# Another order of the same steps in a landmark-attention and two-MLP kernel on one core

## The chip, the core and the metric

The kernel runs on one core of one Trainium2 chip. The metric is the device time of one execution in microseconds (us). The engines are TensorE (PE; its weight loads are shown as PEld), VectorE (DVE), ScalarE (ACT), GpSimd (POOL) and SyncE (SP, which issues the loads). Each engine works off its own queue of instructions in the order in which they were issued, and waits on semaphores for the others.

## What is computed

Landmark attention over 4 batches of 8 heads (576 positions, width 64), then a gated MLP, then an MLP with Mish:

```python
q_lm, k_lm = mean over 18 positions each of q, k          # 32 landmarks
A, Bm, C = sm(q, k_lm), sm(q_lm, k_lm), sm(q_lm, k)        # sm: softmax of scaled scores
Z = Bm.T / (norm1(Bm) * norminf(Bm) + 1e-6)
for _ in range(6):
    Z = 2 * Z - Z @ Bm @ Z
x = (A @ Z @ C @ v)                                        # 2304 tokens x 512
h = ((x @ w1) * (x @ w2)) @ w3 @ w_out                     # 1024 wide
g = mish(h @ w_in)                                         # 2048 wide
out = g @ w_out2
```

## The kernel before

Weights come from memory as 64-bit floats and are decoded on the chip to 32 bits. Everything ahead of the Mish part is cut into 1614 named steps. Each step is declared once with its engine, the steps that it must follow, the buffers that it takes and frees, and a function that emits its instructions. The string `ORDER` (lines 24 to 148) lists the names in one sequence; `issue()` walks it, gives each step the buffer that was freed first, and emits it. So `ORDER` sets the order of each engine's queue, which step gets which buffer, and, where a step has a choice (`@ACT`, `@DVE`, `@POOL`), on which engine it runs. A step whose buffer was used before waits for the last step that used it. The Mish part (`p2`, `z_mm`, `o_mm`, `tick`) comes after the string and is not in it.

The names, with the lines that carry them:

- `ld u` loads a weight tile (512 KB of 64-bit words) into one of seven raw buffers, on SP. It is decoded by `da` (top bits, ACT line 201 or DVE line 203), `dm` (sign, DVE line 207), `ds` (rescale, ACT line 210) and `db` (join, DVE line 214). `wo0` to `wo7` and `w30` to `w315` are the output and the third weight of the gated MLP, `w000` to `w171` its first and second, `x0` to `x25` those of the Mish part. `hi` and `lo` split a tile into a rounded part and a rest.
- `mm n x` multiplies a tile of w3 with one of wo (line 356, two matmuls); sixteen n of four x make the product w3 @ w_out in eight accumulators. Only two banks serve these until the last `mm`, so `mm 4 0` takes the bank of the first accumulator, which `ehi 0` (ACT) and `elo 0` (DVE, line 223) empty, and so on for `mm 8` and `mm 12`.
- `lk`, `lq`, `lv` load K, Q and V of a batch. `ks`, `qs` sum over 18 positions: for batch 0 on DVE (`ks3`, `qs3`, `ks4`, `qs4`, line 409), for the others on POOL as a tree of adds (lines 417, 420, 423). `bdk0` to `bdq3` (lines 432, 434) lay the sums out for the scores.
- A: `as` scores (line 450), `amx`, `asb`, `aex`, `asm`, `aad`, `arc`, `amul` the softmax, `atr` transposes (line 506), `ahi`, `alo` the split (line 223). C: `cs` scores (line 528), `cm`, `cex`, `cad`, `crc`, `ctr`, `cev`, `cv` (line 587), `cve`. Bm and its inverse: `bs` (line 611) to `btr`, `ns0` to `npy1`, then `bp` and `nm`, `nu` in turn (line 646 on TensorE, line 703 on DVE). `lt` and `lte` make Z @ C @ v. The number after the space is the batch. Five banks are shared by `as`, `cs`, `atr`, `ctr`, `cv` and `lt`; one serves `bs`, `bp` and `nm`.
- `m b s` folds that into w1 and w2 for 128 columns (line 850), with `mh`, `ml` splitting it; `xa`, `xb` multiply with A (lines 189 to 191, three matmuls for each product of split parts), `xc` and `xm` (line 886) multiply the two. `sh`, `sl` split the result, `y u m` multiplies with w3 @ w_out (24 matmuls, half a batch u), `ye` copies it out. `yh`, `yl` split it for the Mish part. `swap` ends the attention's buffers.

## Time and profile before

| | us |
|---|---|
| median of 3 runs | 779.53 (776.64 to 779.83) |
| the profiled execution | 776.88 |
| its span in the trace | 775.1 |
| TensorE busy | 750.3 (97%) |
| DVE busy | 350.4 (45%) |
| ACT busy | 337.6 (44%) |
| POOL busy | 120.1 (15%) |

The views used are the page (busy time, the chain that ended last, the groups), the busy time and granted TensorE clock of single stretches, and the instructions of one engine in order of time. A clock of 1.00 is the upper of its two levels (2.4 GHz), 0.50 the lower (1.2 GHz); a value between is a stretch with both. In a line of the order of time, the bracket says how long the engine stood idle ahead of it and what ended that. Ends of matmuls are modelled, so neighbours overlap a little in the list. Times are from the span's start.

### The profile page before, as it was taken

What the parts mean: (1) busy time and instruction counts of PE and PEld (TensorE: products, weight loads), DVE (VectorE), ACT (ScalarE), POOL (GpSimd) and SP (SyncE); (2) the same over time, 40 slices, a digit from 0 to 9 for tenths busy, and PEclk for the clock granted to TensorE, in tenths of its full rate; (3) what the DMA queues carried; (4) which work ended last, traced back from release to release, by engine and by line L of the source; (5) the groups of instructions that cost most, each with busy time, mean ns of one, the idle gap of its engine ahead of it and who ended that gap; (6) DMA issues with size and microseconds to landing.
All of it is one profiled execution on the core that took longest, in us unless ns stands there. A gap on an engine that the chain in (4) does not pass through costs nothing.

```text
span 775.1 us, 13036 instructions
## 1 busy us (share of the span) xinstructions
PE 750.3 (97%) x5188; PEld 616.3 (80%) x5188; DVE 350.4 (45%) x706; ACT 337.6 (44%) x737; POOL 120.1 (15%) x120
## 2 busy tenths in 40 slices
...
GB/s 312 369 329 106 80 192 167 256 127 83 117 114 72 110 55 98 140 117 137 30 107 28 1 0 55 1 0 1 55 0 1 1 0 55 1 0 1 55 1 27
DMA packets 38381, 65.92 MB, mean 85 GB/s; under 512 B 3888, under 2 KB 20400, under 8 KB 38320
## 3 DMA queue, kind: packets, MB, share of 16 engines
...
## 4 chain that ended last, share of the span: by engine, by line
PE 91%; DVE 5%; DMA 2%; issue 1%; ACT 1%; POOL 0%; SPq 0%; DVEq 0%; POOLq 0%
PE ps L189 26%; PE ps L191 26%; PE ps L190 26%; PE ps L356 6%; PE ps L850 2%; PE ps L450 1%; DVE raw L207 1%; DMA raw<-in_wo_dram 1%; PE ps L646 1%; DVE raw L214 1%; PE ps L528 1%; PE ps L587 1%; DMA k<-in_kT_dram 1%; PE ps L566 1%; PE ps L506 0%
## 5 line engine op out<-in xcount | busy, mean ns | idle before, releaser
L1101 ACT ACTIVATE emx<-ps 128x512 f32<-128x512 f32 (+1 forms) x80 | 44.3, 554 | 131.6 <-PE ps L191 131.6
L1103 DVE TENSOR_TENSOR gx<-emx,gx 128x512 fp32r<-128x512 f32 (+1 forms) x40 | 25.6, 639 | 158.6 <-ACT gx L1102 158.6
L189 PE MATMUL ps<-hs,W 128*128 128x288 f32 (+2 forms) x304 | 92.7, 305 | 0.0
L190 PE MATMUL ps<-hs,W 128*128 128x288 f32 (+2 forms) x304 | 92.4, 304 | 0.0
L191 PE MATMUL ps<-hs,W 128*128 128x288 f32 (+2 forms) x304 | 92.2, 303 | 0.0
L207 DVE TENSOR_SCALAR raw<-raw 128x512 uint16<-128x512 uint16 x84 | 74.4, 917 | 37.6 <-ACT raw L201 37.2
L1103 DVE TENSOR_TENSOR hs<-emx,hs 128x512 fp32r<-128x512 f32 (+1 forms) x40 | 25.6, 639 | 136.6 <-ACT hs L1102 136.6
L189 PE MATMUL ps<-AT,M 128*128 128x288 f32 x256 | 78.3, 306 | 1.0 <-DVE M L223 0.9
L190 PE MATMUL ps<-AT,M 128*128 128x288 f32 x256 | 75.6, 295 | 0.0
L191 PE MATMUL ps<-AT,M 128*128 128x288 f32 x256 | 75.5, 295 | 0.0
L210 ACT ACTIVATE raw<-raw 128x512 f32<-128x512 f32 x84 | 55.8, 678 | 29.8 <-DVE raw L207 25.6
L356 PE MATMUL ps<-wo,raw 128*128 128x512 f32 x128 | 61.9, 643 | 5.7 <-DVE raw L214 5.7
L201 ACT ACTIVATE raw<-raw 128x512 int32<-128x512 uint16 x79 | 52.7, 673 | 24.2 <-DMA raw<-in_w_dram 10.5
L190 PEld LDWEIGHTS ps<-hs,W 128*128 128x128 f32 x304 | 57.5, 189 | 1.4
L189 PEld LDWEIGHTS ps<-hs,W 128*128 128x128 f32 x304 | 57.1, 188 | 1.8 <-ACT y L218 0.4
L191 PEld LDWEIGHTS ps<-hs,W 128*128 128x128 f32 x304 | 57.5, 189 | 1.2
L356 PEld LDWEIGHTS ps<-wo,raw 128*128 128x128 f32 x128 | 26.6, 212 | 38.2 <-issue 28.6
L189 PEld LDWEIGHTS ps<-AT,M 128*128 128x128 f32 x256 | 48.1, 188 | 8.2 <-issue 2.1
L1102 ACT ACTIVATE gx<-ps 128x512 fp32r<-128x512 f32 (+1 forms) x40 | 22.2, 556 | 61.2 <-PE ps L190 61.2
L190 PEld LDWEIGHTS ps<-AT,M 128*128 128x128 f32 x256 | 48.1, 188 | 0.0
L191 PEld LDWEIGHTS ps<-AT,M 128*128 128x128 f32 x256 | 48.1, 188 | 0.0
L1102 ACT ACTIVATE hs<-ps 128x512 fp32r<-128x512 f32 (+1 forms) x40 | 22.3, 557 | 54.7 <-PE ps L190 54.7
...
## 6 DMA issues: line engine op xcount, KB each, us to landing
raw<-in_w_dram SPq DMA_DIRECT2D x128, 128.0 KB, 2.6
raw<-in_wo_dram SPq DMA_DIRECT2D x22, 512.0 KB, 4.4
...
raw<-in_wi_dram SPq DMA_DIRECT2D x14, 512.0 KB, 3.9
...
```

The costliest lines, as they stand in the source:

```text
L189: T.matmul(out=o, lhsT=lh, rhs=rh, start=first, stop=False)
L190: T.matmul(out=o, lhsT=lh, rhs=rl, start=False, stop=False)
L191: T.matmul(out=o, lhsT=ll, rhs=rh, start=False, stop=last)
L201: S.activation(w[..., 0], q[..., 1], ACTF.Copy, scale=2.0 ** -13, bias=2.0 ** -14 - 0.5)
L207: V.tensor_scalar(q[..., 1], q[..., 3], 0x8000, None, op0=ALU.bitwise_and)
L210: S.activation(f32(w[..., 1]), f32(w[..., 1]), ACTF.Copy, scale=2.0 ** -112)
L214: V.scalar_tensor_tensor(to, w[..., 1], 3, w[..., 0], op0=ALU.logical_shift_left, op1=ALU.bitwise_or)
L356: T.matmul(out=got(f"acc{i}"), lhsT=f32(got(f"w3{n}")[:, o:o + 128, 0]), rhs=WO0[j // 4][:, j % 4], start=j == 0, stop=j == 7)
L850: T.matmul(out=got(f"p{c}{key}")[32 * i:32 * i + 32, 0:256], lhsT=LT[r, b, 2 * c + par, :], rhs=w12(f"w{bp}{s}{c}")[r, par * 256:par * 256 ...
L1101: S.activation(x, zt[n], ACTF.Mish)
L1102: S.activation(gb(n, 0), zt.pop(n), ACTF.Mish)
L1103: V.tensor_tensor(gb(n, 1), x, f32(gb(n, 0)), op=ALU.subtract)
```

## The change

The string `ORDER` is replaced. The 1614 steps are the same, with the same work in each and the same rules of what must follow what; their sequence is another from the 21st on, and 35 of them run on another engine: 20 `lo` and 7 `sl` go from POOL to DVE, 2 `sl` from DVE to POOL, 2 `sh` from ACT to POOL, `da wo6` from DVE to ACT, `da x6` from ACT to DVE, and `bdq1 3` and `bdq2 3` change places on ACT and POOL. As buffers are given out in the order of the string, many steps also get another bank or buffer. SP's loads are the same; of the first 36, `lk0 2` and `lk1 2` come ahead of `ld w34`, and `lv 1` ahead of `ld w36`. The `y` of the first two batches (u = 0 to 3, but for the last of them, `y 3 3`) now come ahead of `m 2 2`, where before `y 2` and `y 3` stood behind all `xa`; `y 3 3` and `y 4` to `y 7` come behind them.

The sequence at the start, at the first `y`, where `m 2 2` stands, and at the end:

```diff
-    "da wo0@ACT,dm wo0,da wo1@ACT,ds wo0,dm wo1,db wo0,ds wo1,da w30@ACT,ld wo5,db wo1,dm w30,da wo2@ACT,ld w32,"
-    "ds w30,dm wo2,db w30,ds wo2,da wo3@ACT,mm 0 0,db wo2,dm wo3,da w31@ACT,mm 0 1,ds wo3,dm w31,mm 0 2,db wo3,"
-    "ds w31,da wo4@ACT,mm 0 3,ld wo6,ld wo7,db w31,dm wo4,mm 1 0,ld w33,ks3 0,ds wo4,mm 1 1,db wo4,mm 1 2,qs3 0,"
-    "mm 1 3,ks4 0,ld w34,ld w35,bdk0 0@ACT,bdk1 0@ACT,qs4 0,bdk2 0@ACT,bdk3 0@ACT,as0 0,bdq0 0@ACT,bdq1 0@ACT,"
-    "bdq2 0@ACT,bdq3 0@ACT,bs 0,amx0 0,cs0 0,bmx 0,bsb 0,asb0 0,by 0,cs1 0,bsm 0,aex0 0,bad 0,brc 0,bml 0,btr 0,"
-    "ns0 0,bp 0,ns1 0,lk0 2,lk1 2,nc 0,as1 0,ntr 0,nx 0,nml 0,nad 0,nrc 0,npy0 0,npy1 0,cm00 0,nm0 0,cm10 0,nu0 0,"
-    "cm20 0,nm1 0,cm01 0,ks0 1,cex00 0,nu1 0,cm11 0,cex10 0,nm2 0,cm21 0,as2 0,nu2 0,cex01 0,amx1 0,cex11 0,nm3 0,"
-    "asb1 0,lq0 2,lq1 2,ctr0 0,ks1 1,nu3 0,aex1 0,asm0 0,ctr1 0,da wo5@ACT,amx2 0,nm4 0,ks2 1,asm1 0,cev00 0,"
-    "nu4 0,ks3 1,cev10 0,asb2 0,nm5 0,da w32@ACT,ks4 1,cv0 0,nu5 0,dm wo5,aex2 0,cev01 0,dm w32,ds wo5,da wo6@DVE,"
-    "ds w32,db wo5,cev11 0,da wo7@ACT,cv1 0,db w32,ld w36,bdk0 1@ACT,lv 1,bdk1 1@ACT,dm wo6,mm 2 0,bdk2 1@ACT,"
-    "da w33@ACT,dm wo7,mm 2 1,ds wo6,dm w33,ds wo7,db wo6,mm 2 2,ds w33,db wo7,da w34@ACT,mm 2 3,db w33,ld w37,"
-    "ld w38,da w35@ACT,dm w34,mm 3 0,ld w39,bdk3 1@ACT,dm w35,ds w34,mm 3 1,cad0 0,ds w35,db w34,mm 3 2,crc0 0,"
-    "qs0 1,asm2 0,cve0 0,mm 3 3,ehi 0,elo 0,lt0 0,ehi 1,ld w310,as0 1,qs1 1,lte0 0,elo 1,db w35,mm 4 0,cad1 0,"
-    "crc1 0,qs2 1,amx0 1,cve1 0,mm 4 1,aad0 0,arc0 0,qs3 1,aad1 0,da w36@ACT,arc1 0,mm 4 2,amul0 0,mm 4 3,dm w36,"
...
-    "bsm 1,cm00 1,bdk2 2@ACT,bdk3 2@ACT,cm10 1,cm20 1,mm 8 1,qs1 2,asb0 1,cex00 1,amx1 1,mm 8 2,cex10 1,asb1 1,"
-    "qs2 2,aex0 1,mm 8 3,amx2 1,aex1 1,qs3 2,asm0 1,mm 9 0,ld w315,qs4 2,asm1 1,bdq0 2@ACT,mm 9 1,db w312,"
...
-    "ml1 2 2,xa 3 1 0,sl 0 7@DVE,sh 1 2@POOL,xm 2 1 0,xb 3 1 0,dm w150,sh 1 3@POOL,xc 2 1 1,y 0 0,ds w150,dm w151,"
...
-    "ld x24,ld x25,da x22@ACT,dm x22,y 7 0,yh 0,yh 1,yl 0,yh 2,yl 1,yh 3,yl 2,da x23@ACT,yl 3,da x24@ACT,dm x23,"
-    "y 7 1,ds x22,dm x24,da x25@ACT,db x22,ds x23,dm x25,ds x24,db x23,y 7 2,ds x25,db x24,ye 6 3,ye 7 0,db x25,"
-    "ye 7 1,y 7 3,ye 7 2,ye 7 3"
...
+    "da wo0@ACT,dm wo0,da wo1@ACT,ds wo0,dm wo1,da w30@ACT,db wo0,ds wo1,dm w30,ld wo5,da wo2@ACT,db wo1,ds w30,"
+    "dm wo2,ld w32,da wo3@ACT,db w30,ds wo2,dm wo3,mm 0 0,da w31@ACT,db wo2,ds wo3,mm 0 1,dm w31,da wo4@ACT,"
+    "mm 0 2,db wo3,ds w31,dm wo4,mm 0 3,ld wo6,ld wo7,ks3 0,ds wo4,ld w33,qs3 0,ks4 0,db w31,bdk0 0@ACT,"
+    "bdk1 0@ACT,qs4 0,bdk2 0@ACT,mm 1 0,bdk3 0@ACT,mm 1 1,db wo4,bdq0 0@ACT,bdq1 0@ACT,mm 1 2,bdq2 0@ACT,"
+    "bdq3 0@ACT,bs 0,cs0 0,bmx 0,bsb 0,by 0,bsm 0,bad 0,cs1 0,brc 0,bml 0,btr 0,ns0 0,ns1 0,nc 0,bp 0,ntr 0,lk0 2,"
+    "lk1 2,mm 1 3,nx 0,nml 0,nad 0,nrc 0,ks0 1,cm00 0,as0 0,ld w34,ld w35,cm10 0,cm20 0,cm01 0,cex00 0,cm11 0,"
+    "cm21 0,cex10 0,as1 0,npy0 0,cex01 0,npy1 0,cad0 0,crc0 0,ks1 1,amx0 0,cex11 0,asb0 0,da wo5@ACT,nm0 0,ks2 1,"
+    "amx1 0,da w32@ACT,ctr0 0,nu0 0,aex0 0,ctr1 0,ks3 1,asb1 0,cev00 0,ks4 1,nm1 0,asm0 0,cev10 0,as2 0,qs0 1,"
+    "da wo6@ACT,nu1 0,da wo7@ACT,nm2 0,amx2 0,lq0 2,lq1 2,cv0 0,aex1 0,nu2 0,asb2 0,da w33@ACT,nm3 0,asm1 0,qs1 1,"
+    "cve0 0,nu3 0,cev01 0,nm4 0,cev11 0,nu4 0,aex2 0,qs2 1,cv1 0,bdk0 1@ACT,asm2 0,bdk1 1@ACT,nm5 0,cad1 0,"
+    "bdk2 1@ACT,lv 1,crc1 0,qs3 1,bdk3 1@ACT,nu5 0,cve1 0,dm wo5,as0 1,da w34@ACT,dm w32,ds wo5,dm wo6,ds w32,"
+    "lt0 0,db wo5,lt1 0,lte0 0,db w32,lte1 0,ld w36,as1 1,ds wo6,dm wo7,da w35@ACT,db wo6,ds wo7,mm 2 0,dm w33,"
+    "db wo7,mm 2 1,ds w33,dm w34,ld w37,ld w38,mm 2 2,db w33,ds w34,mm 2 3,dm w35,db w34,mm 3 0,ds w35,ld w39,"
+    "da w36@ACT,aad0 0,qs4 1,arc0 0,mm 3 1,amx0 1,amul0 0,bdq0 1@ACT,amx1 1,mm 3 2,da w37@ACT,bdq1 1@ACT,mm 3 3,"
+    "db w35,bdq2 1@ACT,da w38@ACT,dm w36,atr0 0,ld w310,bdq3 1@ACT,as2 1,dm w37,ahi0 0,ds w36,bs 1,dm w38,ds w37,"
+    "db w36,ds w38,db w37,da w39@ACT,db w38,da w310@ACT,dm w39,ehi 0,dm w310,ehi 1,ds w39,aad1 0,ks0 2,arc1 0,"
+    "alo0 0,ds w310,bmx 1,cs0 1,bsb 1,elo 0,by 1,bsm 1,elo 1,mm 4 0,amul1 0,cm00 1,mm 4 1,cm10 1,ks1 2,cm20 1,"
+    "asb0 1,mm 4 2,cex00 1,amx2 1,cex10 1,mm 4 3,db w39,aex0 1,mm 5 0,ld w311,db w310,mm 5 1,aad2 0,arc2 0,ks2 2,"
...
+    "xa 3 1 0,xm 2 1 0,xb 3 1 0,sl 0 7@DVE,sh 1 1@POOL,xc 3 1 0,y 0 0,sl 1 0@DVE,sh 1 2@POOL,xm 2 0 1,sl 1 1@DVE,"
...
+    "sl 3 7@DVE,y 2 3,ye 2 2,y 3 0,sh 4 0@ACT,sh 4 1@ACT,sl 4 0@DVE,ye 2 3,sl 4 1@DVE,y 3 1,ye 3 0,m 2 2,ye 3 1,"
...
+    "lo x18@DVE,ld x21,yh 0,lo x19@DVE,yh 1,ld x22,yh 2,yl 0,ld x23,ld x24,ld x25,yh 3,yl 2,da x20@ACT,yl 1,y 7 1,"
+    "ye 5 3,yl 3,ye 6 0,da x21@ACT,dm x20,ye 6 1,dm x21,ds x20,da x22@ACT,db x20,y 7 2,ds x21,dm x22,da x23@ACT,"
+    "db x21,ds x22,da x24@ACT,dm x23,db x22,ds x23,y 7 3,da x25@ACT,dm x24,ye 6 3,db x23,ds x24,dm x25,ye 7 0,"
+    "ye 7 1,db x24,ds x25,ye 7 2,db x25,ye 7 3,ye 6 2"
```

## Rows read from the trace of the kernel before

**Rows 1.** The page: span, busy time by engine, chain that ended last.

```profile
span 775.1 us, 13036 instructions
...
PE 750.3 (97%) x5188; PEld 616.3 (80%) x5188; DVE 350.4 (45%) x706; ACT 337.6 (44%) x737; POOL 120.1 (15%) x120
...
PE 91%; DVE 5%; DMA 2%; issue 1%; ACT 1%; POOL 0%; SPq 0%; DVEq 0%; POOLq 0%
```

**Rows 2.** By stretch: span; PE, PEld, DVE, ACT, POOL busy; clock; DMA share; GB/s.

```profile
13.48:43.07 29.59, 22.78 (x283) 14.80 (x283) 26.90 (x54) 15.31 (x40) 11.10 (x9) 0.86 1.05 377
...
61.75:80.06 18.31, 13.43 (x67) 8.06 (x65) 17.40 (x20) 12.37 (x26) 12.91 (x10) 0.88 0.27 82
...
80.06:118.55 38.49, 37.48 (x298) 18.91 (x299) 27.59 (x71) 21.10 (x47) 2.66 (x3) 0.97 0.45 137
...
118.55:227.69 109.14, 106.95 (x1408) 89.61 (x1405) 88.61 (x224) 69.53 (x184) 30.78 (x36) 1.00 0.47 146
...
227.69:377.80 150.11, 150.11 (x1247) 143.79 (x1246) 87.30 (x169) 90.30 (x198) 37.86 (x38) 1.00 0.30 99
```

**Rows 3.** TensorE in order of time: start, length, line, operands, count, idle before.

```profile
13.48 8.84 PE L356 MATMUL ps<-wo,raw 128*128 128x512 f32 x16 [4.62 <-DVE raw L214]
...
30.11 0.42 PE L646 MATMUL ps<-py 32*32 32x64 f32 x16 [0.50 <-DVE py L703]
...
41.59 0.44 PE L587 MATMUL ps<-vt,et 64*32 64x64 f32 x8 [3.40 <-ACT et L577]
...
43.07 9.74 PE L356 MATMUL ps<-wo,raw 128*128 128x512 f32 x16 [1.04 <-DVE raw L214]
...
77.10 1.01 PE L450 MATMUL ps<-bdk,q 128*64 128x64 f32 x7 [4.88 <-DVE AT L223]
...
80.06 15.19 PE L356 MATMUL ps<-wo,raw 128*128 128x512 f32 x32
...
96.56 14.01 PE L356 MATMUL ps<-wo,raw 128*128 128x512 f32 x32
...
114.59 0.42 PE L646 MATMUL ps<-py 32*32 32x64 f32 x16 [0.41 <-DVE py L703]
```

**Rows 4.** Single microseconds of TensorE: busy time, clock.

```profile
14.00:15.00 1.00, 1.00 (x3) 0.61 1.04 396
...
31.00:32.00 1.00, 1.00 (x23) 0.64 0.97 375
...
81.00:82.00 1.00, 1.00 (x3) 0.50 0.00 0
```

**Rows 5.** Busy time by stretch, 30 to 52 us: the rate of the DMA.

```profile
30.00:52.00 22.00, 16.10 (x193) 9.50 (x194) 17.98 (x33) 13.77 (x33) 11.10 (x9) 0.77 1.05 375
```

**Rows 6.** DVE in order of time.

```profile
17.50 1.32 DVE L409 TENSOR_REDUCE sumk<-k 128x64 f32<-128x1152 f32 x1
...
36.38 4.29 DVE L207 TENSOR_SCALAR raw<-raw 128x512 uint16<-128x512 uint16 x2
...
42.94 1.91 DVE L207 TENSOR_SCALAR raw<-raw 128x512 uint16<-128x512 uint16 x3
...
52.62 0.69 DVE L223 TENSOR_TENSOR W<-ps,W 128x512 fp32r<-128x512 f32 x1 [3.59 <-ACT W L218]
```

**Rows 7.** POOL in order of time.

```profile
30.27 2.39 POOL L417 TENSOR_TENSOR tree<-k 128x1152 f32<-128x1152 f32 x1 [28.48 <-DMA k<-in_kT_dram]
...
36.11 2.40 POOL L417 TENSOR_TENSOR tree<-q 128x1152 f32<-128x1152 f32 x1
```

**Rows 8.** ACT in order of time.

```profile
45.46 1.27 ACT L201 ACTIVATE raw<-raw 128x512 int32<-128x512 uint16 x2
```

**Rows 9.** The page, DMA issues: count, KB each, median us to landing.

```profile
raw<-in_wi_dram SPq DMA_DIRECT2D x14, 512.0 KB, 3.9
```

**Rows 10.** ACT and DVE alone in the last four groups of `y`.

```profile
327.00:377.80 50.80, 32.33 (x69) 1.00 0.33 110
...
327.00:377.80 50.80, 27.59 (x50) 1.00 0.33 110
```

200 rows, old and new, of the table ORDER are left out of this document.

## The prediction, made before the changed kernel ran

> **What bounds the kernel now.** I read the page first: TensorE is busy 97% of a span of 775.1 us and makes up 91% of the chain that ended last [rows 1]. So the reader should not look for a cheaper operation. The steps are the same before and after; only two things can change: the time in which TensorE stands still and the time in which it runs at half clock. Next the stretches [rows 2]: from 227.7 us on TensorE never stops and its clock is 1.00; from 118.6 to 227.7 it stops 2.2 us; the mish part begins at 377.8. What can be won lies ahead of 118.6 us, where the mean clock is 0.86 to 0.97 and TensorE stands still 6.8 us from 13.5 to 43.1, 4.9 us from 61.8 to 80.1 and 1.0 us from 80.1 to 118.6. Then the order of TensorE's work there [rows 3], to see each stop and what ended it, and the clock around the stops [rows 4].
>
> A matmul step `mm` is two matmuls; 32 of them take 14.01 us at full clock [rows 3], so 0.86 us a step after their overlap. Pricing every step at the pace that its kind shows at full clock, I get 46.5 us of TensorE work between the first `mm` (13.48) and `mm 8 0` (80.06), which is 66.6 us later: 20 us are lost there. They are: 1.8 us of half clock behind the idle time 8.86 to 13.48; 9 us in the attention of batch 0, of which 3.4 and 1.0 are the two stops ahead of `mm 2 0` (43.07); 2.7 us of half clock behind those (16 matmuls in 9.74 us); 4.9 us ahead of 77.10, and 1.2 us of half clock before 80. Another 1.3 us of half clock follow in the first 32 matmuls behind 80.06 (15.19 against 14.01). Between `mm 12 0` and the second set of `xa` 4 us more go in small stops, all else later is 7.6 us, spread thin.
>
> Two things hold the early part. DMA moves 375 GB/s from 30 to 52 us with its engines fully busy [rows 5], so weights can't come sooner, whatever the order. And DVE is a queue: `dm` is 0.73 us alone, but the two at 36.38 took 4.29, because POOL's adds ran at the same time, one of 2.40 us from 36.11 and the next ones behind it [rows 6, 7].
>
> **The change, part by part.** I laid the new order out by hand with these durations; back to back, decode steps follow each other by 0.6 us on ACT (two in 1.27) and on DVE (three in 1.91) [rows 6, 8].
>
> *Up to `mm 0 3`* nothing of weight moves: 18.7 us as before. *`db w31`* is moved behind the three sums `ks3`, `qs3`, `ks4` of batch 0. Each is 1.33 us and they start at 17 us [rows 6], so `db w31` ends at 21.9 instead of 17.1, and `mm 1 0` waits for it: a new stop of 3.2 us. Behind it on DVE stand `qs4 0` and `db wo4`, which lose nothing by it: the sums are the same 5.3 us in both orders. Three `mm` then stand where `as0 0` stood, and `bs 0` comes at 24.5 (before: 24.0), so batch 0's small chain is not delayed by more than 0.5.
>
> *Batch 0's chain* runs on with `as0 1`, `lt0 0`, `lt1 0` and `as1 1` pulled ahead of `mm 2 0`, 4.3 us of work in the place of the long stop. ACT is now threaded with `da` steps that wait for landings (one weight tile each 1.4 us at 375 GB/s [rows 5, 9]), and everything on ACT behind them waits too. Counting bytes from the load that landed at 30.2 [rows 7], w34 lands at 42.6; `da w34`, `ds wo5`, `ds w32`, `lte0 0` end at 44.6; `as1 1` writes the bank that `lte0 0` frees, so it runs 44.65 to 46.6. DVE's decode of wo5 and w32 comes after POOL's adds and is done by 45.2. `mm 2 0` is at 46.6 with 23.0 us of work behind it: 10.1 us lost, before 10.8.
>
> *`mm 2` to `mm 4 0`.* `mm 2` and `mm 3` end at 53.5, `atr0 0` and `as2 1` at 54.5. `bs 1` needs `bdq3 1`, which ACT has behind `da w38`; w38 lands at 54.6 to 55.1 by bytes, so `bs 1` is at 55.6 (1.1 us lost). `cs0 1` takes the bank that `alo0 0` frees and `mm 4 0` the one that `elo 0` frees. Before, `elo 0` and `elo 1` stood right behind their `ehi` at 52.6 and 53.5 and cost nothing [rows 6, 8]; now both `elo` stand behind `dm w39`, `dm w310`, `alo0 0`, `bmx 1` and `bsb 1`. ACT: `ahi0 0`, three `ds`, two `da` from 55.6 at 0.6 make 59.1; DVE then `dm w310` 59.9, two small ones 60.3, `alo0 0` 61.0, two more, `elo 0` 62.0. So a stop from 55.9 to 61.0, and half clock behind it. The row for that price is the stop of 4.9 us before 77.10, which cost 1.2 and 1.3: I take 2.4 (ends: 0, and 2.7 as behind 43.07).
>
> *`mm 4` to `mm 8`.* 13.7 us of `mm`, and `atr1 0`, `atr2 0`, `bp 1` of 1.0, with no stop: `elo 2` follows `ehi 2` directly, and the bank of `as2 1`, whose late release was the 4.9 us before, is free early. 62.1 + 2.4 + 14.7 = 79.2 for `mm 8 0`, against 80.06 with 0.5 us less work behind it. The half clock behind 80 (1.3) goes, about 0.4 of small waits come: **2.3 us ahead at `mm 9`**.
>
> *`mm 12` to the second `xa`.* Of the 4 us lost there before, 1.7 are the chain `nm1` to `nm5` of batch 1 with nothing between, and 1.5 the same of batch 2 [rows 3]. The new order puts `nm0 1` ahead of `mm 12` and `xa` steps between most others; two stops of 0.5 stay, and two smaller: I take 1.9 us. **2.1 us ahead.**
>
> *The rest.* From there to 227.7 DVE is busy 88.6 us of 109 and ACT 69.5 [rows 2]; TensorE sets the pace in both orders. I cost the new order of `xa`, `xb`, `m` at 0, ends -2 and +3. The four `y` groups of the first two batches now come ahead of the other `xa`; their `sh` stay 12.7 us a group behind TensorE. 27 `lo` and `sl` go from POOL to DVE, off the path, and cost nothing while DVE has 27.6 of 50.8 us in use at the end [rows 10].
>
> Sum: 2.3 + 2.1 = 4.4 us. The profiled execution took 776.88 (span 775.1 and 1.8 around it): 772.5. It stands at the lower end of the runs (776.64, 779.53, 779.83); from the median the same sum gives 775.1. I take **774.0**.
>
> **Rivals.**
> *A. The clock stays low.* The new stop of 3.2 us lies between stops after which the clock fell (3.4 and 1.0; 4.6; 4.9) and short ones. For it: the clock fell in 31 to 32 us where no stop was over 0.6 us, only thin small matmuls [rows 3, 4], and the new order has thin work from 32 to 41. Then `mm 1` costs 1.7 more and `as1 1` and `mm 2` up to 2.7. Against: 1.1 us of the first are swallowed by the wait for w38, and before paid 2.7 at the same place. Net 2 to 4 us lost of the 4.4: 776 to 779. The Trainium skill says the same of short pauses ("TensorE: Matmul & The Clock Gate", section "A second HAM failure mode: psum-queue depth-cycling": frequent brief pauses between matmul groups make the clock go back and forth); the row at 31 us agrees, and by that rule this rival would be the likeliest.
>
> *B. The decode of the mish weights comes too late: slower.* Six more of the `x` tiles are now decoded and split behind `y 3 3`. By my count ACT then has 50 us of instructions, one after the other, in the 50.8 us of `y 4` to `y 7`, where it was busy 32.3 before, and DVE 48 where it was 27.6 [rows 10]. The price: four rounds of loads (`x8`, `x12`, `x16`, `x20`) each hold the ACT queue until a load lands (3.9 us [rows 9]); if each round holds it 3 us, ACT ends 11 us late; the first `z_mm` writes the bank that `ye 6 3` frees, some 3.7 us are covered, 7.5 are lost. It decides from 1.1 us a round if ACT's instructions don't overlap. For it: there is no slack by full durations. Against: back to back they follow each other by 0.60 where one is 0.67 [rows 8], so 50 is 45, and the `sh` of the next half stand behind each `ld`. 776.9 - 4.4 + 7.5 = 780, to 785.
>
> *C. The new order of the middle gives it back.* It moves hundreds of steps between 113 and 215 us in three in-order queues; the order of before loses 7 us there, the new one may lose 10 to 12. 776 to 779.
>
> *D. The early stops are shorter than I laid out* (`elo 0` is the tail of a queue of eleven steps; each microsecond is one of TensorE's): 766 to 770.
>
> **How the numbers follow.** Forecast 0.45 (770 to 777), A 0.18, B 0.12, C 0.15, D 0.10. The likeliest is the forecast. A measurement here tells 0.5%, 3.9 us, from no change. Of the forecast 0.32 is faster by more and 0.13 within; A gives 0.02, 0.12, 0.04; B 0, 0.04, 0.08; C 0.01, 0.08, 0.06; D all faster. Together 0.45 faster, 0.37 same, 0.18 slower. Range 767 to 783: it takes in A and C, most of D and the lower part of B.
>
> **What the profile afterwards would show.** Right: TensorE stops of 3 us ahead of the ninth `mm` pair (about 22 us), of some 5 us ended by DVE (line 223) near 61 us, and none at 72 to 77; `mm 2 0` near 46.6, `mm 8 0` near 79, mish at 373. Wrong, A: clock 0.50 between 22 and 26 and again behind 46. B: TensorE idle behind 373, released by ACT. C: stops between 113 and 215 that add up to more than 7 us. The step that I trust least is the walk of ACT and DVE from 55 to 62 us.

## The result: slower by 0.6%, and the profile after

The changed kernel takes 781.06 us (median of 22 runs, 777.63 to 784.31) against 776.67 for the kernel before (22 runs, 774.56 to 779.83): a ratio of 1.0056, 95% interval 1.0042 to 1.0071. I had forecast 2.9 us less than the 776.88 of the profiled execution; it is 4.4 us more, median against median. The profiled execution of the changed kernel took 778.92, so its profile shows 2.0 of these 4.4 us; a second profile (780.45) shows more of the rest.

The page of the changed kernel, its span, busy times and the chain that ended last (before: [rows 1]):

```profile
span 777.1 us, 13027 instructions
...
PE 750.3 (97%) x5188; PEld 613.9 (79%) x5188; DVE 352.4 (45%) x731; ACT 336.0 (43%) x735; POOL 87.2 (11%) x97
...
PE 87%; DMA 5%; DVE 3%; SPq 2%; ACT 1%; issue 1%; POOL 1%; DVEq 0%; ACTq 0%; POOLq 0%
```

TensorE's busy time is 750.3 as before. In the chain DMA has grown from 2% to 5% and TensorE has shrunk from 91% to 87%: more of the end hangs on loads.

Its stretches, cut at the same steps as [rows 2] where the order allows it: span; PE, PEld, DVE, ACT, POOL busy; clock; DMA share; GB/s:

```profile
13.71:48.50 34.79, 29.52 (x331) 19.31 (x331) 27.99 (x60) 18.92 (x51) 10.97 (x10) 0.83 1.04 374
48.50:64.91 16.41, 10.21 (x47) 4.78 (x46) 14.94 (x28) 11.11 (x22) 5.49 (x4) 0.85 0.58 167
64.91:80.73 15.82, 15.82 (x57) 7.47 (x55) 11.35 (x28) 6.29 (x16) 8.66 (x10) 0.94 0.39 115
...
117.53:229.28 111.75, 109.02 (x1439) 89.93 (x1439) 82.55 (x209) 67.82 (x175) 21.06 (x28) 1.00 0.36 115
229.28:379.80 150.52, 150.52 (x1262) 144.07 (x1261) 101.97 (x199) 91.21 (x200) 11.28 (x18) 1.00 0.32 109
```

The stop of 4.9 us before 80 is gone (15.82 of 15.82 busy). In its place TensorE stands still 6.2 us between 48.5 and 64.9, while DMA, on the mean of that stretch, moves only 167 GB/s. Behind 229.28 it never stops.

TensorE of the changed kernel in order of time (columns as in [rows 3]):

```profile
13.71 6.32 PE L356 MATMUL ps<-wo,raw 128*128 128x512 f32 x8 [5.85 <-DVE raw L214]
22.09 4.55 PE L356 MATMUL ps<-wo,raw 128*128 128x512 f32 x6 [2.05 <-DVE raw L214]
...
34.59 2.34 PE L450 MATMUL ps<-bdk,q 128*128 128x64 f32 x16 [2.42 <-ACT ce L547]
...
48.50 7.09 PE L356 MATMUL ps<-wo,raw 128*128 128x512 f32 x16
...
58.44 0.31 PE L611 MATMUL ps<-sumk,bdq 128*64 128x32 f32 x4 [1.71 <-ACT bdq L432]
...
63.75 1.23 PE L528 MATMUL ps<-k,bdq 128*64 128x288 f32 x4 [4.49 <-DVE AT L223]
64.91 14.93 PE L356 MATMUL ps<-wo,raw 128*128 128x512 f32 x32
```

`mm 1 0` comes at 22.09, `mm 2 0` at 48.50 and at full clock (16 matmuls in 7.09; 9.74 in [rows 3]), `mm 4 0` at 64.91 behind stops of 1.7 and 4.5 us.

Priced as in the prediction (each step of TensorE at its full-clock pace), the time lost since the first `mm`, in us:

| profile | at `mm 9` | at `xa 0 1 0` | at `y 0 0` | at `y 7 3` | execution |
|---|---|---|---|---|---|
| before | 21.4 | 25.4 | 30.7 | 33.0 | 776.88 |
| changed | 20.2 | 25.2 | 32.7 | 34.8 | 778.92 |
| changed, second profile | 20.8 | 25.6 | 34.8 | 36.9 | 780.45 |

So 1.2 us were won by `mm 9` (forecast: 2.3), 1.0 went back by `xa 0 1 0`, where I had written 2.1 won, and 2.1 (3.8 in the second) were lost from there to `y 0 0`, where I had written zero. With 0.2 us by which the first `mm` started later, that is the 2.0.

### The profile page after: what moved, and what is told of

Read it like the earlier page. It is cut to its first block, busy times and chain, and to the rows that moved or that the text cites. A ratio compares the mean times of both kernels' runs of the same rounds, so it can differ in the third digit from the quotient of the medians.

```text
span 777.1 us, 13027 instructions
## 1 busy us (share of the span) xinstructions
PE 750.3 (97%) x5188; PEld 613.9 (79%) x5188; DVE 352.4 (45%) x731; ACT 336.0 (43%) x735; POOL 87.2 (11%) x97
## 4 chain that ended last, share of the span: by engine, by line
PE 87%; DMA 5%; DVE 3%; SPq 2%; ACT 1%; issue 1%; POOL 1%; DVEq 0%; ACTq 0%; POOLq 0%
PE ps L189 25%; PE ps L191 25%; PE ps L190 25%; PE ps L356 6%; PE ps L850 2%; DMA raw<-in_w3T_dram 2%; DMA raw<-in_w_dram 1%; DMA k<-in_kT_dram 1%; SPq L825 1%; PE ps L646 1%; DMA q<-in_qT_dram 1%; PE ps L450 1%; PE ps L528 1%; DVE raw L207 1%; PE ps L506 1%
## 5 line engine op out<-in xcount | busy, mean ns | idle before, releaser
L1103 DVE TENSOR_TENSOR gx<-emx,gx 128x512 fp32r<-128x512 f32 (+1 forms) x40 | 25.6, 639 | 151.3 <-ACT gx L1102 151.3
L207 DVE TENSOR_SCALAR raw<-raw 128x512 uint16<-128x512 uint16 x84 | 69.0, 852 | 37.4 <-ACT raw L201 37.1
L201 ACT ACTIVATE raw<-raw 128x512 int32<-128x512 uint16 x79 | 53.4, 679 | 52.4 <-DMA raw<-in_w_dram 22.5
L190 PEld LDWEIGHTS ps<-hs,W 128*128 128x128 f32 x304 | 57.4, 189 | 1.4
L191 PEld LDWEIGHTS ps<-hs,W 128*128 128x128 f32 x304 | 57.4, 189 | 1.3
L190 PEld LDWEIGHTS ps<-AT,M 128*128 128x128 f32 x256 | 48.1, 188 | 0.0
L191 PEld LDWEIGHTS ps<-AT,M 128*128 128x128 f32 x256 | 48.1, 188 | 0.0
```

Of the source, the lines that this page charges most:

```text
L190: T.matmul(out=o, lhsT=lh, rhs=rl, start=False, stop=False)
L191: T.matmul(out=o, lhsT=ll, rhs=rh, start=False, stop=last)
L201: S.activation(w[..., 0], q[..., 1], ACTF.Copy, scale=2.0 ** -13, bias=2.0 ** -14 - 0.5)
L207: V.tensor_scalar(q[..., 1], q[..., 3], 0x8000, None, op0=ALU.bitwise_and)
L1103: V.tensor_tensor(gb(n, 1), x, f32(gb(n, 0)), op=ALU.subtract)
```

## The experiments

Each is numbered as it ran, and the expectations count that way ("the third-last" in number 10 is number 6).

### Where the time goes, and why it varies

**0. The changed kernel again.** No edit.

> The changed kernel once more, unchanged. Its profiled execution (778.92) lies 2.1 us under the median of its runs (781.06), and its runs went from 777.6 to 784.3 while the mean granted clock went from 0.988 to 0.980. Theory: what differs from run to run is how long TensorE stays at half clock in the early part, so a slower profile shows more half clock between 13 and 70 us and else nothing; ratio again about 1.005. Rival: the spread sits elsewhere (loads that land later), and the clock of the early part is the same in a slower profile.

781.83 us, ratio 1.0051 (1.0033 to 1.0070). The slower profile is not slower in the early part: it loses 0.5 us more up to `mm 9`, and 1.7 us more in the middle. So the theory fell, and the rival fits this pair: nearly all of the 1.7 us is time in which TensorE stands still in the middle (3.4 us instead of 1.6, rows under number 11). Its longest stop there, 1.5 us ahead of `xa 0 2 1`, is ended by ACT, where `da w070`, ahead of an `xc` that frees the bank, stands 3.5 us at its load (2.1 in the first profile). But the early part does vary too, as five more profiles show in which it is the same instruction for instruction. The six matmuls of `mm 1 0` to `mm 1 2`, behind the new stop, in the second profile, and in the profile of the experiment with the middle moves (below):

```profile
21.54 2.85 PE L356 MATMUL ps<-wo,raw 128*128 128x512 f32 x6 [3.00 <-DVE raw L214]
```
```profile
21.77 5.49 PE L356 MATMUL ps<-wo,raw 128*128 128x512 f32 x6 [3.00 <-DVE raw L214]
```

The same six behind the same stop of 3.00 us: at full clock in 2.85, at half clock in 5.49, in the first profile (stop 2.05) in 4.55. What hangs on it: batch 0's small chain comes at different times beside POOL's adds. In the first profile one of its smallest steps met them (DVE, then POOL, from the changed kernel):

```profile
30.41 2.28 DVE L678 TENSOR_SCALAR cc<-cc 128x2 f32<-128x2 f32 x1
...
54.11 3.52 DVE L207 TENSOR_SCALAR raw<-raw 128x512 uint16<-128x512 uint16 x2
...
64.00 0.68 DVE L223 TENSOR_TENSOR W<-ps,W 128x512 fp32r<-128x512 f32 x1
```
```profile
30.29 2.38 POOL L417 TENSOR_TENSOR tree<-k 128x1152 f32<-128x1152 f32 x1 [28.50 <-DMA k<-in_kT_dram]
...
53.60 2.87 POOL L417 TENSOR_TENSOR tree<-k 128x1152 f32<-128x1152 f32 x1
```

`nad 0`, two elements a partition and 0.17 us in the second profile, took 2.28 and ended with POOL's add; that is the stop of 2.42 ahead of `as1 0`. The Trainium skill ("SBUF — State Buffer", section "SBUF: two separate sides") says that VectorE, in some kinds of operation, and GpSimd share a pair of ports, and that whichever starts first holds it as an exclusive lock for its whole instruction. The rows agree: POOL's add started first, at 30.29, and `nad 0` ended with it, at 32.69; whether `nad 0` is of those kinds no run here shows. With the six matmuls wholly at half clock, two steps of the chain met adds (2.2 and 2.1 us), and `mm 2 0` came at 51.7 to 52.0 instead of 48.1 to 49.0. Over six profiles with this early part the loss at `mm 9` was 20.2, 20.8, 22.4, 24.9, 25.2 and 25.2, on the mean 23.1. Before's order is steadier: up to `mm 7 0`, where five other profiles hold it unchanged or nearly so, 12.9 to 13.9 against 13.7. On the mean the early part thus loses 1.7 us against the one profile of before, where the first profile, the best of the six, wins 1.2.

**1. The join ahead of the sums.** One step moved back.

```diff
-ks3 0,ds wo4,ld w33,qs3 0,ks4 0,db w31,bdk0 0@ACT
+db w31,ks3 0,ds wo4,ld w33,qs3 0,ks4 0,bdk0 0@ACT
```

> The changed kernel with the join of w31 back ahead of the three sums of batch 0, so that mm 1 0 follows mm 0 3 at once. Theory: the stop of 2.2 us ahead of mm 1 and the half clock behind it go (mm 1 at 19 instead of 22), and, as batch 0's chain comes earlier, nad 0 no longer runs beside POOL's first add (2.3 us). But as1 1 still waits for the load of w34 and mm 4 0 for the load of w38: mm 2 0 comes 1 to 2.5 us earlier, mm 4 0 at most 1. So 0 to 1.5 us under the changed kernel. Rival: each of the 5 to 7 us lost there is one of the whole: 774 to 776.

781.41, ratio 1.0048 (1.0031 to 1.0066): nothing won, as the theory had it. Its TensorE:

```profile
13.18 7.69 PE L356 MATMUL ps<-wo,raw 128*128 128x512 f32 x14 [5.10 <-DVE raw L214]
...
64.59 1.23 PE L528 MATMUL ps<-k,bdq 128*64 128x288 f32 x4 [4.06 <-DVE AT L223]
65.75 9.56 PE L356 MATMUL ps<-wo,raw 128*128 128x512 f32 x16
```

`mm 1` follows `mm 0` at once and `as0 0` comes 3.6 us earlier. But `mm 2 0`, which I had 1 to 2.5 us earlier, comes at 49.77 in this profile, later than 48.50, and `mm 4 0` at 65.75, behind the same wait. The loss at `mm 9` is 23.1, the mean of the six. So the new stop, taken alone, is covered by later ones.

**2. The split of the first accumulators early.** `ehi`, `elo`, `ahi0`, `alo0` and `bdq3 1` ahead of the decode of w38.

```diff
-mm 3 3,db w35,bdq2 1@ACT,da w38@ACT,dm w36,atr0 0,ld w310,bdq3 1@ACT,as2 1,dm w37,ahi0 0
...
-dm w39,ehi 0,dm w310,ehi 1,ds w39,aad1 0,ks0 2,arc1 0,alo0 0,ds w310,bmx 1,cs0 1,bsb 1,elo 0,by 1,bsm 1,elo 1
+mm 3 3,db w35,bdq2 1@ACT,bdq3 1@ACT,ehi 0,ehi 1,atr0 0,elo 0,elo 1,ahi0 0,alo0 0,da w38@ACT,dm w36,ld w310,as2 1
...
+dm w39,dm w310,ds w39,aad1 0,ks0 2,arc1 0,ds w310,bmx 1,cs0 1,bsb 1,by 1,bsm 1
```

> The changed kernel with ehi 0, ehi 1, elo 0, elo 1, ahi0 0, alo0 0 and bdq3 1 ahead of the decode of w38 instead of behind it and that of w39 and w310. Theory: the stop ahead of mm 4 0 (5.2 us, and 1 us of half clock behind it) shrinks to 1 us: mm 4 0 near 59 instead of 64.9, mm 8 0 near 75, the end 4 to 6 us under the changed kernel, 774 to 777. Rival: the loads behind it (w311 and later are issued when mm 4 3 is done) or batch 1's chain give the time back before mm 12: mm 8 0 earlier, the end within 1.5 us of the changed kernel.

777.49, ratio 1.0004 (0.9990 to 1.0018): 4 us under the changed kernel. TensorE:

```profile
59.13 0.71 PE L528 MATMUL ps<-k,bdq 128*64 128x288 f32 x4 [0.96 <-DVE AT L223]
59.77 14.01 PE L356 MATMUL ps<-wo,raw 128*128 128x512 f32 x32
...
77.90 1.13 PE L356 MATMUL ps<-wo,raw 128*128 128x512 f32 x2 [3.17 <-DVE W L223]
```

`mm 4 0` at 59.77 and at full clock (14.01 for 32). Then `mm 8 0` waits 3.17 us for `elo 2`, which stands behind the decode of w312 on DVE: 5.5 us won at `mm 5`, 2.2 left at `mm 9` against the first profile. The theory held for `mm 4 0` (59) and for the time within half a microsecond, not for `mm 8 0` (77.9 instead of 75).

**4. The load of w34 behind the chain.** `da w34` waits for a landing on ACT with `lte0 0` and the rescale of wo5 behind it.

```diff
-as0 1,da w34@ACT,dm w32,ds wo5,dm wo6,ds w32,lt0 0,db wo5,lt1 0,lte0 0,db w32,lte1 0
+as0 1,dm w32,ds wo5,dm wo6,ds w32,lt0 0,db wo5,lt1 0,lte0 0,db w32,lte1 0,da w34@ACT
```

> The changed kernel with one step moved: da w34 (ACT) stands behind lte1 0 instead of ahead of ds wo5, ds w32 and lte0 0. Theory: in the second profile of the changed kernel batch 0's chain was done at 40.2, but ACT stood at da w34 until w34 landed (42.6), and with it lte0 0 (the bank of as1 1) and the rescale of wo5, whose tile frees the raw buffer for the load of w36. With the step moved as1 1 starts at 42 to 43 instead of 44.7, w36 is issued 2 us earlier, w38 lands near 55 instead of 57.4, and mm 4 0 comes 2 us earlier: 779 to 780. Rival: another wait (the kept stop ahead of mm 4 0) takes all of it: 781 to 782.

782.63, ratio 1.0064 (1.0041 to 1.0087). In its profile `mm 2 0` came at 45.97 and `mm 4 0` at 62.19, 1.5 to 2.7 us earlier as the theory had it. The whole was no faster: in this profile the clock fell from 118 to 125 us and took about 3 us.

**3 and 8. The two orders joined at `mm 8 0`.** The first kernel has the changed string up to `mm 8 0` and then the tokens of before's string that are left, in their order; the second the other way round (with `lt1 0` seven tokens later, when its bank is free).

> Up to mm 8 0 the changed order, from there the steps that are left in the order of before. Theory: in the profiles the early part of the changed order is 0.9 us ahead at mm 9 and the order behind it loses 2.9 us more than that of before; so the profile of this one is near 776, and its median 2 us above that if the runs spread in clock as those of the changed kernel do. Rival: the early part alone makes the changed kernel slower: 780 to 782; or the early part is harmless and the median is as that of before, 776 to 777.

> The mirror of the third experiment: up to mm 8 0 the order of before, from there the steps that are left in the changed order. Theory: the changed order loses 3 to 4 us more than that of before between xa 0 1 0 and y 0 0 (7.3 to 9.6 us in the profiles that hold it, 5.4 to 6.0 in those with the order of before), so this kernel is 3 to 4 us over before: 780 to 782, and ACT stands 13 us or more at the loads of w1 and w2 between 120 and 216. Rival: the whole loss is made ahead of mm 8, and this kernel is as before: 777 to 778.

781.37, ratio 1.0059 (1.0037 to 1.0081), and 786.02, ratio 1.0111 (1.0085 to 1.0136). The totals say less than I hoped: at the joint, work stands in an order that fits neither half, and the second loses 5.9 us between `mm 8 0` and `mm 9` alone. What can be read is the stretch far behind the joint. From `xa 0 1 0` to `y 0 0` the first loses 5.5 us, the second 8.6. With before's order there, seven profiles lost 5.4 to 6.9, on the mean 6.2; with the changed order untouched there, six lost 7.4 to 9.6, on the mean 8.7. So the loss in the middle belongs to the order: 2.5 us on the mean.

### What the middle waits for

**5. Four moves in the middle.** Steps of the product (`xc`, `xm`) ahead of four decode steps and of a copy that wait.

```diff
-da w070@ACT,xm 1 1 0,xb 1 1 1,ds w061,dm w070,xa 0 2 0,xc 1 1 1,amx1 2
+xm 1 1 0,xb 1 1 1,xa 0 2 0,xc 1 1 1,da w070@ACT,ds w061,dm w070,amx1 2
...
-da w111@ACT,xm 1 3 1,aad2 2,xb 0 4 0,xc 0 4 0
+xm 1 3 1,aad2 2,xb 0 4 0,xc 0 4 0,da w111@ACT
```

> The changed kernel with four small moves between 137 and 178 us, none ahead of that: xm 1 0 0 ahead of dm w051 and xc 0 1 0 ahead of da w060; da w070, ds w061, dm w070 behind xc 1 1 1; bdq0 3 behind xc 1 2 0; da w111 behind xc 0 4 0. Theory: TensorE's small stops there (0.4 to 1.7 us each, before xb 0 1 0, xa 0 2 1, xb 1 2 1 and xa 0 4 1) come from xc and xm standing on ACT and DVE behind decode steps that wait for a load, or behind a copy that waits for POOL. They go, and the loss from xa 0 1 0 to y 0 0 falls from 9 to 6 or 7 us: 1.5 to 3 us under the changed kernel, 778.5 to 780. Rival: the stops are set by something else (the decode itself is late) and come back a step later: no change, 781 to 782.

783.47, ratio 1.0058 (1.0028 to 1.0089): no gain; the loss there is 8.5. The stops ahead of `xa 0 2 1`, `xb 1 2 1` and `xa 0 4 1` are gone, others of 0.5 to 1.0 stand ahead of `m 1 2`, `xb 0 2 1` and `xa 0 3 1`: each wait went on to the next step of the same queue.

**11. Half loads.** The loads of w1 and w2 leave out w2, so part of the input is not loaded.

```diff
-            for i, w in enumerate((w1, w2)):
+            for i, w in enumerate((w1,)):
```

> The changed order, but the loads of w1 and w2 bring only the half that belongs to w1 (64 of 128 transfers are left out, so part of the input is not loaded); every step stays. Theory: ACT stands at loads that have not landed and holds xc, mh and the rest behind it; with loads that land 1.5 us earlier its time at loads between 120 and 216 us falls from 13 to 16 us to under 7, and the loss from xa 0 1 0 to y 0 0 from 7.3 to 9.6 us to about 6: 778 to 779. Rival: that loss is set by the order of ACT's and DVE's own work, and stays: 781 to 782.

776.82, ratio 1.0002 (0.9982 to 1.0022): 4 to 5 us come back. The loss from `xa 0 1 0` to `y 0 0` is 5.3, TensorE stands still 0.24 us there instead of 1.6 to 3.4. The stretch in before, in the changed kernel, in its second profile and with half loads (columns as in [rows 2]):

```profile
140.38:227.69 87.31, 85.40 (x1049) 73.47 (x1048) 70.81 (x171) 55.57 (x143) 30.78 (x36) 1.00 0.41 132
138.22:229.28 91.06, 89.44 (x1106) 74.25 (x1104) 66.90 (x172) 54.86 (x142) 21.06 (x28) 1.00 0.35 111
138.01:230.82 92.81, 89.40 (x1106) 74.35 (x1105) 66.94 (x172) 54.61 (x142) 20.75 (x28) 1.00 0.36 110
144.38:233.28 88.90, 88.66 (x1105) 74.16 (x1104) 66.73 (x172) 54.01 (x141) 20.75 (x28) 1.00 0.23 70
```

So the stops there hang on loads. But before has such stops too: 1.9 to 2.5 us in the seven profiles with its order, on the mean 2.2, against 2.6 in the six with the changed one. Of the 2.5 us that the changed order loses more, 0.4 lie in stops; half loads also take away stops that before has. The rest is time in which TensorE counts as busy (see number 16; ends of matmuls are modelled, so part of a wait can hide in it).

**12. Decode later.** All loaded; `da`, `dm`, `ds` of ten tiles (`w040` to `w111`) some 12 tokens later, for example

```diff
-da w070@ACT,xm 1 1 0,xb 1 1 1,ds w061,dm w070,xa 0 2 0,xc 1 1 1,amx1 2,ds w070,xb 0 2 0,xm 1 1 1,xc 0 2 0,asb1 2,xa 0 2 1
+xm 1 1 0,xb 1 1 1,xa 0 2 0,xc 1 1 1,amx1 2,xb 0 2 0,xm 1 1 1,xc 0 2 0,asb1 2,da w070@ACT,xa 0 2 1
```

> The changed order with da, dm and ds of ten tiles (w040 to w111) 12 steps later in the string, db where it was; the order of TensorE, POOL and the loads is untouched. Nothing is left out. Theory: what the half loads gave back (4.5 us in all, 2 to 4 of it between xa 0 1 0 and y 0 0) was the time for which ACT and DVE stand at loads with xc, xm, mh behind; with the steps later ACT stands under 6 us there instead of 13 to 16, the loss in that stretch falls from 7.3 to 9.6 to 5.5 to 6.5, the whole to 778 to 779. Rival: the half loads helped because less was decoded late or because DMA was free for other loads: no change, 781 to 782.

780.53, ratio 1.0034 (1.0015 to 1.0052): about 1 us, and 9.1 lost in the stretch, so the theory fell. What ACT waited for from 138 to 216 us, first before, then the changed kernel, the half loads and the decode later (count; busy, mean ns; idle before and its releaser; L201 is `da`, L432 the copy `bdq`):

```profile
L201 ACT ACTIVATE raw<-raw 128x512 int32<-128x512 uint16 x14 | 9.3, 671 | 3.2 <-DMA raw<-in_w_dram 3.2
```
```profile
L201 ACT ACTIVATE raw<-raw 128x512 int32<-128x512 uint16 x13 | 8.8, 678 | 11.4 <-DMA raw<-in_w_dram 11.3
L432 ACT ACTIVATE bdq<-sumq 64x64 f32<-64x64 f32 x3 | 0.8, 254 | 1.8 <-POOL sumq L423 1.8
```
```profile
L201 ACT ACTIVATE raw<-raw 128x512 int32<-128x512 uint16 x15 | 10.0, 676 | 2.0 <-DMA raw<-in_w_dram 1.9
```
```profile
L201 ACT ACTIVATE raw<-raw 128x512 int32<-128x512 uint16 x14 | 9.5, 678 | 5.2 <-DMA raw<-in_w_dram 5.2
L432 ACT ACTIVATE bdq<-sumq 64x64 f32<-64x64 f32 x3 | 0.8, 256 | 3.3 <-POOL sumq L423 3.2
```

The changed order has ACT stand 11.3 us at loads where before had 3.2. With the decode later that is 5.2, but the copy `bdq0 3` now waits 3.2 us for POOL's sums of Q of batch 3, with `xc 1 2 0` behind it, and TensorE stops 1.6 us ahead of `xb 1 2 1`. That Q is loaded from 147 us on in the changed order, from 140 in before.

The string also moves loads that I did not put back in any run. V of batch 2 and K of batch 3 are issued at 100.5 and 102.5 us instead of 119.9 and 136.8, ahead of `ld w011`; the tile `w040` is issued at 124.9 instead of 111.9, and `w120`, which waits for a `db` to free its buffer, at 197.4 instead of 177.2. That these cause the waits at loads is a rival that stays open.

**16. The queries out of the way too.**

```diff
-ml0 0 3,bdq0 3@ACT,lt0 2,xc 1 2 0,xa 1 2 1,bdq1 3@ACT
+ml0 0 3,lt0 2,xc 1 2 0,xa 1 2 1
...
-xm 1 2 0,xc 1 2 1
+xm 1 2 0,xc 1 2 1,bdq0 3@ACT,bdq1 3@ACT
```

(`cev01 2` stands ahead of `ds w060` again.)

> The twelfth experiment (ten tiles' decode later) with three steps more: bdq0 3 and bdq1 3 (ACT) behind xc 1 2 1 and cev01 2 ahead of ds w060. Theory: with the decode later ACT no longer stood at loads (5.2 us), yet the loss stayed at 9.1, because the next wait in ACT's queue took its place: bdq0 3, with xc 1 2 0 behind it, waits for POOL's sums of Q of batch 3, whose load came 7 us later than in before. With both out of the way the loss from xa 0 1 0 to y 0 0 falls to 6 to 7 us and the time to 777.5 to 779. Rival: DMA itself is the limit there (only the half loads freed it), and again another wait comes: 780 to 781.

779.02, ratio 1.0024 (1.0006 to 1.0043); 7.5 us lost in the stretch. That is 1.5 us under number 12 in both, and short of the 6 to 7 that I wrote. But the two intervals overlap, and a loss of 7.5 lies among the 7.4 to 9.6 of the untouched order, so that both waits counted is not shown. Some of the excess is in no stop. TensorE's groups of line 189 there, first before, then changed:

```profile
L189 PE MATMUL ps<-AT,M 128*128 128x288 f32 x140 | 42.3, 302 | 1.0 <-DVE M L223 0.9
```
```profile
L189 PE MATMUL ps<-AT,M 128*128 128x288 f32 x140 | 43.4, 310 | 0.8 <-DVE h L886 0.3 <-ACT a L218 0.2
```

The mean of the same 140 matmuls is 8 ns higher, 1.1 us in all, in every profile with the changed order there (308 to 311 against 302 to 305). The traces show where that comes from. A matmul of line 189 that follows one of another kind takes about 0.40 us, one that follows its own kind 0.29, as these two of the changed kernel do:

```profile
132.74 0.40 PE L189 MATMUL ps<-AT,M 128*128 128x288 f32 x1
133.25 0.29 PE L189 MATMUL ps<-AT,M 128*128 128x288 f32 x1
```

In that stretch 19 of them follow another kind in the changed order, 11 in before; those behind their own kind take the same in both (294 to 298 ns). Eight more such changes at 0.1 us are 0.8 of the 1.1 us. That part belongs to the order and stays with half loads (19 too).

### What stops ahead of 118 us are worth

**7. All moves together**, on the changed order: the join, `da w34`, the early split, the middle moves, and `ehi 2`, `elo 2` right behind `mm 7 2`.

> The changed kernel with all moves tried on it: db w31 back ahead of the sums, da w34 behind the chain, ehi, elo, ahi, alo early as in e2, the middle moves, and ehi 2 and elo 2 right behind mm 7 2 ahead of the decode of w311 and w312. Theory: the waits that were covered by one another go together: as e2 (777.5) less 2 for the middle, 3 for the stop that e2 had ahead of mm 8 0, and 2 for the early part: 769 to 772. Rival: the early part stays bound by the loads, and only the middle and mm 8 0 count: 772 to 775.

776.40, ratio 0.9989 (0.9971 to 1.0007): 4 to 5 us better than the changed kernel, level with before. The twelve runs went from 774.46 to 781.02; the profile is the last of these, with the clock at 0.50 from 116 to 126 us.

**13. The early split and the later decode together.**

> The same ten tiles later, on top of ehi, elo, ahi, alo early as in the second experiment (777.5). Theory: the two waits lie in different stretches and add: 777.5 less 2.5 to 3.5, so 774 to 775, under before. Rival: they do not add, because what is won ahead of mm 8 only brings the chain of batch 2 sooner to the same loads: 777.

778.23, ratio 1.0011 (0.9992 to 1.0029). They do not add: the rival was right. `mm 8 0` waits 3.2 us as in the early split alone, and the middle still loses 8.3.

**15. Every mend**: the seventh with the later decode, and `ehi 3`, `elo 3`, `ehi 6` early too.

> The changed order with every mend: db w31 ahead of the sums, da w34 behind batch 0's chain, ehi, elo, ahi, alo early, elo 2 and elo 3 right behind mm 7, and the ten tiles later. Theory: the seventh experiment (776.4) less the 2 to 3 us that its middle moves left: 773 to 775; where the clock falls behind 115 us it is 4 to 5 us more in single runs. Rival: as the seventh, 776 to 777.

778.21, ratio 1.0014 (0.9998 to 1.0030), no better. The changed order, mended, comes to before and not under it.

**6. Before's order with its own stop removed.** Does a stop taken away ahead of 80 us come back as time?

```diff
-dm w310,mm 7 1,ds w39,dm w311,ds w310,mm 7 2,db w39
+dm w310,mm 7 1,ds w39,alo0 0,alo1 0,dm w311,ds w310,mm 7 2,ehi 2,elo 2,db w39
```

> The order of before with four steps moved: alo0 0 and alo1 0 ahead of the decode of w311 on DVE, ehi 2 right behind mm 7 2 and elo 2 ahead of db w39. Theory: the stop of 4.9 us ahead of as2 1 goes nearly whole, and most of the 2.5 us of half clock behind it; what is won there stays, since from there on neither loads nor decode set the pace: 4 to 7 us under before, 770 to 773. Rival: loads or the chain of batch 1 take it back before m 0 0: 775 to 777.

781.79, ratio 1.0056 (1.0035 to 1.0076): slower than before, by as much as the change. Its TensorE, and its clock behind 114 us:

```profile
75.70 1.23 PE L528 MATMUL ps<-k,bdq 128*64 128x288 f32 x4 [3.40 <-DVE AT L223]
76.86 7.38 PE L356 MATMUL ps<-wo,raw 128*128 128x512 f32 x12
```
```profile
114.00:128.00 14.00, 13.42 (x196) 9.26 (x197) 8.52 (x32) 5.80 (x20) 0.00 (x0) 0.53 0.57 163
```

`as2 1` waits no more, but the second half of `cs0 1` waits for the bank that `alo2 0` frees; 2.1 us were left at `mm 9`. Then the clock fell, from 115 to 128, and 5.7 us more than in before were lost between `mm 9` and `xa 0 1 0`. In before the same chain with the same stops (0.41 us, [rows 3]) runs at 1.00.

**10 and 14. Two ways on from there.** The first moves `alo2 0` too and threads `nm0` to `nm5` of batch 1 between `mm 13` and `mm 15`; the second moves `alo2 0` and `elo 3` and leaves the chain.

```diff
-elo 6,nm0 1,ld w031,widen,ctr0 1,nu0 1,atr0 1,db w020,cev00 1,nm1 1
...
+dm w001,mm 13 1,nm0 1,nu0 1
...
+mm 13 3,nm1 1
...
+mm 14 3,nm2 1,nu2 1
```

> The order of before with alo0 0, alo1 0, alo2 0 and elo 2 ahead of the late decode steps (so that neither as2 1 nor cs0 1 nor mm 8 0 waits), and with the chain nm0 to nm5 of batch 1 threaded into mm 13 to mm 15 instead of bare behind them. Theory: the stop of 4.9 us and the half clock behind it go, the chain's stops of 0.5 us go, and with them the fall of the clock that the third-last experiment had from 115 to 128 us: 8 us less, 768 to 772. Rival: the clock falls there also without these stops, since the work is thin: 774 to 778.

```diff
-mm 7 2,db w39,ds w311,db w310,mm 7 3,da w312@ACT
+mm 7 2,ehi 2,elo 2,ds w311,db w310,mm 7 3,ehi 3,atr2 0,ahi2 0,alo2 0,elo 3,db w39,da w312@ACT
```

> The order of before with alo0, alo1, alo2 of batch 0, elo 2 and also elo 3 ahead of the late decode steps, the chain of batch 1 bare as in before. Theory: in the tenth experiment the stop ahead of mm 8 0 had only moved to mm 8 1, which takes the bank that elo 3 frees; with elo 3 early it goes, and the loss at mm 9 falls from 21.4 to 14 to 15. If the clock then holds from 112 to 130 us, 769 to 771; if it falls there as in the sixth experiment, 774 to 776. Rival: DVE's decode, late behind POOL's adds, stops mm 9 or mm 10 instead: 777 or more.

781.40, ratio 1.0043 (1.0019 to 1.0068), and **774.33, ratio 0.9955 (0.9936 to 0.9974)**: the second beats both kernels. In the first, `mm 8 1` now waits 3.6 us for the bank that `elo 3` frees, and its profile has the clock down behind 118 us; four of its twelve runs are at 776.6 to 776.9 with a mean clock of 0.986 to 0.987, eight at 781.1 to 784.2 with 0.975 to 0.980. The second:

```profile
72.94 14.01 PE L356 MATMUL ps<-wo,raw 128*128 128x512 f32 x32
...
91.17 5.33 PE L356 MATMUL ps<-wo,raw 128*128 128x512 f32 x8 [2.84 <-DVE W L223]
```
```profile
106.00:127.00 21.00, 19.71 (x429) 14.37 (x428) 16.76 (x53) 15.07 (x41) 0.00 (x0) 1.00 0.56 167
```

`mm 8 0` comes at 72.94 instead of 80.06 and 32 matmuls follow in 14.01. Of the 8.2 us won at `mm 9`, 4.5 go back at `mm 12`, which waits for `elo 4` and runs at half clock behind it. The thin stretch holds its clock, 1.6 more go in the middle, and 2.1 us reach the end of this profile, 3.4 us the medians: not the 769 to 771 that I wrote for a clock that holds.

**17. The same mend one stage on**: `ehi 4`, `elo 4` behind `mm 11 2`, `ehi 5`, `elo 5` behind `mm 11 3`, ahead of the decode of w000.

```diff
-mm 11 1,crc0 1,dm w000,mm 11 2,aad0 1,ds w000,arc0 1,aad1 1,arc1 1,amul0 1,asb2 1,mm 11 3,ehi 4,aex2 1,elo 4
+mm 11 1,crc0 1,mm 11 2,ehi 4,elo 4,aad0 1,arc0 1,aad1 1,arc1 1,amul0 1,asb2 1,mm 11 3,ehi 5,elo 5,da w000@ACT,dm w000,ds w000,aex2 1
```

> The fourteenth experiment (before with elo 2, elo 3 and alo early: 774.3) with the same mend one stage later: ehi 4, elo 4, ehi 5, elo 5 right behind mm 11, ahead of the decode of w000. Theory: its profile stopped 2.9 us ahead of mm 12 0, which takes the bank of elo 4, and 1.7 us of half clock followed; both go: 770 to 771. Rival: the clock falls in the thin stretch behind mm 15 instead, as in three kernels that came there early: 774 to 776.

780.25, ratio 1.0035 (1.0020 to 1.0050). The stop ahead of `mm 12 0` fell from 2.84 to 0.75 us, and then:

```profile
107.96 0.42 PE L646 MATMUL ps<-py 32*32 32x64 f32 x16 [1.76 <-DVE py L703]
```
```profile
110.00:127.00 17.00, 15.92 (x251) 10.86 (x247) 10.02 (x33) 7.47 (x23) 0.00 (x0) 0.50 0.58 171
```

The chain waits 1.76 us for `nu0 1`, which stands on DVE behind two decode steps and `elo 6`; the clock falls and stays at 0.50 for 17 us. From `mm 14` to `xa 0 1 0` this profile takes 8.4 us more than that of number 14. All eight runs have a mean clock of 0.976 to 0.980. The rival had the mechanism; the time is 4 us above its range.

**9. The mended early part with before's rest**: the early split and `elo 2` as in the seventh, joined at `mm 8 0`.

> Up to mm 8 0 the changed order with ehi, elo, ahi, alo early and ehi 2, elo 2 right behind mm 7 2; the rest in the order of before. Theory: the early part is then 3 to 5 us ahead of before at mm 9 (loss 17 to 18 instead of 21.4) and the rest costs what it costs in before (11.6 us): 773 to 775. Rival: the clock falls again in the thin stretch ahead of xa 0 0 0, as it did in three kernels that came there earlier, and takes 4 to 5 us: 777 to 779.

780.18, ratio 1.0033 (1.0015 to 1.0052). 16.9 us lost at `mm 8 0`, 24.5 at `mm 9`: at the joint `mm 8 1` waits 4.6 us for a bank, with half clock behind. It decides nothing on the rest.

## Why the prediction was wrong, step by step

**Right.** The base: before's 22 runs have a median of 776.67, next to the 776.88 that I counted from. `db w31` ended at 22.03 (I had 21.9) and `mm 1 0` came at 22.09. w34 landed at 42.5 (42.6). The stop ahead of `mm 4 0` is there, and for the reason given: `alo0 0` and `elo 0` at the tail of DVE's queue. The stop at 72 to 77 is gone. Behind `y 0 0` no more is lost than in before; rival B, late decode of the mish weights, did not occur (TensorE busy 150.52 of 150.52 us from 229.28).

**Wrong: no half clock behind the early stops.** I took none there in the forecast and put it, 1.7 us at `mm 1` and up to 2.7 at `as1 1` and `mm 2`, into rival A. In the first profile `mm 0` ran at half clock to its end (20.04 instead of 18.7) and the six matmuls of `mm 1` took 4.55 instead of the 2.85 of full clock; `bs 0` came at 26.56, I had 24.5. In the second profile `mm 1` was at full clock, `nad 0` met no add, and `as1 1` came at 44.65, just as I had it; but then it ran at half clock, and `mm 2 0` came at 48.12 instead of 46.6 (second profile):

```profile
44.65 3.68 PE L450 MATMUL ps<-bdk,q 128*128 128x64 f32 x16 [1.39 <-ACT LT L218]
```

The rule of the Trainium skill that I weighed there ("TensorE: Matmul & The Clock Gate", section "A second HAM failure mode: psum-queue depth-cycling"), that frequent brief pauses make the clock go to and fro, is not tested by this: the 2.85, 4.55 and 5.49 us for the same six matmuls stand behind one stop of 2 to 3 us, in different executions.

**Wrong: POOL.** I counted `dm` and `db` as the steps that POOL's adds hold up, and did not ask which steps of the chain would now stand beside them. `nad 0` did (2.28 us), and `as1 1` came at 46.66 instead of 44.65, `mm 2 0` at 48.50 instead of 46.6. At 54.1 `dm w36` met the next add (3.52 us for two).

**Wrong: when the queue behind w38 starts.** I had w38 at 54.6 to 55.1 by bytes; in the first profile it landed at 57.4. The load of w36 was issued at 46.86, when `db wo5` freed its buffer, 4.4 us later than in before, w37 and w38 come behind it, and from there to the landing DMA, 97% busy, moved 287 GB/s and not 375. The row of ACT that carries it, in the changed kernel, and the same one in the second profile:

```profile
57.45 0.65 ACT L201 ACTIVATE raw<-raw 128x512 int32<-128x512 uint16 x1 [2.02 <-DMA raw<-in_w3T_dram]
```
```profile
54.88 0.69 ACT L201 ACTIVATE raw<-raw 128x512 int32<-128x512 uint16 x1 [0.38 <-DMA raw<-in_w3T_dram]
```

In the first, `elo 0` started at 64.00 instead of 61.3, and the stop ended 2.8 us after the point that I had computed. In the second, w38 landed at 54.8 as I had it, and the stop still ended 1.6 us late: `mm 2` and `mm 3` ran partly at half clock, `atr0 0` came at 56.39 instead of 53.5, and `ahi0 0`, the head of the same queue, waited for it. From `ahi0 0` on the walk took 6.3 and 6.5 us, where I had 6.4. What the place of the split in that queue cost is shown: moved ahead of it, the split gave 4 us back (number 2).

**Wrong: `mm 12` to the second `xa`.** I had 2.1 us won there; 0.9 were lost, on the mean of the two profiles. Two stops of 0.4 us in the chains stayed, as I had written, but a new one stands ahead of `m 0 0`, which I had not priced, ended by a split on DVE:

```profile
117.53 0.67 PE L850 MATMUL ps<-w,LT 64*32 64x256 f32 x16 [1.42 <-DVE W L223]
```

And a step of the chain that stands between two `xa` steps makes one more change of kind, which I had priced at nothing (number 16).

**Wrong: "the rest at zero".** 2.1 us more than before in the first profile and 3.8 in the second. I had put the term at zero with ends of -2 and +3, the loss as rival C with a chance of 0.15, and had looked only at how busy DVE and ACT were. ACT was busy less than before (67.8 us from 117.5 to 229.3; 69.5 in [rows 2]) and yet held work up, since its queue stood at loads. Half loads removed the stops, so they come from loads that land after the place where the string expects them; which wait in particular is not settled, since each one taken away was followed by another. But of the 2.5 us on the mean only 0.4 lie in more stops, and some 0.8 in eight more changes between kinds of matmul, which I had priced at nothing; for the rest the cause stays open.

**And one execution stood for all.** The early part of the changed order lost 20.2 in the profile and 20 to 25 in others. The forecast's 4.4 us rested on a walk with one time for each clock, load and collision.

On the mean of the profiles the account is: 1.7 us lost in the early part (forecast: 2.3 won), 0.9 from `mm 9` to `xa 0 1 0` (forecast: 2.1 won), 2.5 in the middle (forecast: 0), less 0.2 behind `y 0 0`: 4.9, where 4.4 were measured. All three terms failed. The sets of profiles differ from term to term, and the first two are held against one profile of before.
